# A banded attention and two MLPs in float32: score products without the high-and-low split, other engines for three PSUM copies, one inversion of the softmax sums per pair

## The chip, the cores and the metric

The kernel runs on one core of a Trainium2 chip. That core has a matrix engine (PE in the profile, with its weight loads as PEld), a vector engine (DVE), an activation engine (ACT), a third elementwise engine (POOL) and an engine that issues transfers (SP). Each engine runs its own list of instructions in order, and the lists meet at semaphores. [...]

The metric is the device time of one execution in microseconds, given as the median of several runs. Before the change it is 720.07 us, the median of 3 runs from 719.04 to 720.75 us.

## The reference

```python
def _attn_ref(q, k, v, n_sink, window):        # q, k, v: [2, 8, 768, 64] float32
    scores = scale * np.matmul(q, k.transpose(0, 1, 3, 2))
    keep = is_sink | in_window                 # n_sink = 4, window = 128
    scores = np.where(keep, scores, -1000000000.0)
    scores = scores - np.max(scores, axis=-1, keepdims=True)
    a = np.exp(scores)
    a = a / (np.sum(a, axis=-1, keepdims=True) + 1e-09)
    return np.matmul(a, v)
def _moe_ref(x, w_in, w_out):                  # x: [1536, 512]; w_in [512, 2048]
    h = x @ w_in
    return (h * (1.0 / (1.0 + np.exp(-1.702 * h)))) @ w_out
def _moe2_ref(x, w_gate, w_val, w_out):        # [512, 1536] twice, [1536, 512]
    gate = 1.0 / (1.0 + np.exp(-(x @ w_gate)))
    return (gate * (x @ w_val)) @ w_out
```

The output is the second MLP of the first MLP of the attention's result. The weights come as float64.

## The kernel before

**Products in two formats.** PE takes 4-byte operands in two ways here. In the round format (float32r) an operand carries a shortened mantissa, so the kernel splits a float32 number into a high and a low part and adds three products (high by high, high by low, low by high). In the plain format (float32) one matrix instruction of the program does the whole product. Both MLPs and the scores use the split; the product of the probabilities with v and all transposes are plain.

**Phase A** is the attention. It has 2 batches of 3 query blocks of 256 queries, and each block has 4 pairs of heads, so 24 units. A unit goes through four stages. `st_a` (line 241) transposes q and k of a pair on PE into the PSUM tile `tqk` and brings them to the SBUF tile `kq` of that pair: ACT casts the high part (L255), DVE subtracts it to get the low part (L257), POOL carries the previous block's keys (L246) and the sinks (L259) along. `st_b` (line 262) makes the scores `s` of each half block (`e`) and each head (`j`), with three products each (L278): the two heads of a pair hold 64 rows of PE each. DVE adds the mask and takes the maximum (L283), ACT exponentiates and sums (L291), DVE adds 1e-9 to the sums and inverts them (L294, L295), once for each half block, and POOL scales (L298). `st_c` (line 303) transposes the probabilities (L315) into the PSUM tile `tp`, and ACT copies them to `pt` (L319). `st_d` (line 330) multiplies them with v (L347) and splits the result for the MLP. The first block of a batch has 128 and 256 key columns in its two half blocks, the others 272 each.

**Behind phase A** run the first products of the first MLP, `ha` in `mlp_h` (line 359), one set per block of 256 tokens, and the conversion of weights from float64 (L100 to L108). From some 174 us on, PE does the MLPs alone.

**The order of the work.** The emission order is the string `order` with the four stages at lags 0, 1, 3 and 4 units, but the tile framework reorders it: it simulates a timeline of the whole program and lists each engine's instructions by that. So the lists move wherever an edit changes an instruction's length or engine. PSUM has three buffers for transposes (`ps_t`), three for scores (`ps_s`), one for `o` and one for `ha`.

Of the kernel before, what the change touches and what calls it, by code (L numbers as in the profile page):

```python
# [8 lines left out]
F32 = mybir.dt.float32  # L9
# [6 lines left out]
P = 128  # L16
NS = 16          # sink columns that the banded path carries
NEG = -3.0e38
# the high words of 2^-127 and of the largest float32, both as float64, read as float32
# [19 lines left out]
def fast_path(ctx, tc, ident, nwv, any_, q, k, v, n_sink, window, w_in, w_out, w_gate, w_val, w_out2, out):  # L39
# [5 lines left out]
    KD = DM // P              # 4 contraction tiles of the model dimension  # L45
    TB = 512                  # tokens per MLP block
    NTB = NT // TB
    QB = 256                  # queries per attention block
    NQB = S // QB
    NPAIR = H // 2  # L50
    GF = 4                    # feature tiles per weight group
# [18 lines left out]
    # what the fast path rests on, checked at the end: the sizes of the weights'  # L70
    # exponents, and each row's maximum
# [5 lines left out]
    def weight_block(src, nm, pool):  # L77
        """A block's tiles, and the steps that fill them: float64 words to float32
        (exponent moved, mantissa cut to 24 bits), then hi + lo."""
        wh = pool.tile([P, 4, 512], F32R, tag="wh", name=f"wh_{nm}")  # L80
        wl = pool.tile([P, 4, 512], F32R, tag="wl", name=f"wl_{nm}")

        def load(i):
            raw = stg.tile([P, 512, 2], I32, tag="raw", bufs=2, name=f"raw_{nm}_{i}")
            nc.sync.dma_start(raw, src[:, i, :].bitcast(I32).rearrange("p (f t) -> p f t", t=2))
            return raw

        def steps():
            raws = [load(0)]
            yield  # L90
            for i in range(4):
                if i < 3:
                    raws.append(load(i + 1))
                raw = raws[i]
                lo, hi = raw[:, :, 0], raw[:, :, 1]
                w = stg.tile([P, 512], I32, tag="w", bufs=2, name=f"w_{nm}_{i}")
                wf = w.bitcast(F32)
                n = len(nbig)
                nbig.append(nm)
                nc.scalar.activation(wf, hi.bitcast(F32), AF.Abs, scale=2.0 ** -112,  # L100
                                     accum_out=big[:, n : n + 1])
                yield
                nc.vector.tensor_scalar(w, w, 3, None, ALU.logical_shift_left)
                nc.vector.scalar_tensor_tensor(w, hi, -0x80000000, w, ALU.bitwise_and, ALU.bitwise_or)
                nc.vector.scalar_tensor_tensor(w, lo, 29, w, ALU.logical_shift_right, ALU.bitwise_or)
                yield
                nc.scalar.copy(wh[:, i, :], wf)  # L107
                nc.gpsimd.tensor_tensor(wl[:, i, :], wf, f32(wh[:, i, :]), ALU.subtract)  # L108
                yield

        return (wh, wl), steps()
# [3 lines left out]
    def load_w(src, nm):  # L115
        """The next block, in the slot of the one five before it."""
        w, steps = weight_block(src, nm, wpool if slots[0] % 5 < 3 else wpool2)
        slots[0] += 1
        return w, steps
# [7 lines left out]
    def mm3(ps, ah, al, bh, bl, first, last):  # L127
        """ps += a.T @ b with a = ah + al, b = bh + bl."""
        nc.tensor.matmul(ps, ah, bh, start=first, stop=False)  # L129
        nc.tensor.matmul(ps, ah, bl, start=False, stop=False)  # L130
        nc.tensor.matmul(ps, al, bh, start=False, stop=last)  # L131

    # =====================================================================
    # phase A: attention, with the first weight group behind it
    # =====================================================================
# [31 lines left out]
    def load_vsink(b):  # L167
        """v of the sinks, for the rows (head of the pair, half of the block, sink)."""
        vsk[b] = ap_.tile([4 * NS, NPAIR, 2, D], F32, tag="vsk", bufs=1, name=f"vsk_{b}")
        nc.gpsimd.memset(vsk[b], 0.0)  # L170
        for j in range(2):
            for e in range(2):
                r = (2 * j + e) * NS
                nc.sync.dma_start(vsk[b][r : r + NS, :, e, :],
                                  v[b, j::2, :NS, :].rearrange("h s d -> s h d"))

# [23 lines left out]
    # (their parts stand in a buffer of the probabilities until the masks are made)  # L200
    mt = ap_.tile([P, 2, 2, QB + NS], F32, tag="pr", bufs=2, name="mt").rearrange("p a b c -> p (a b c)")
    rel = mt[:, : QB + P]                             # p - c + 128
# [31 lines left out]
    # keys and queries of a pair of heads, transposed, hi and lo:  # L234
    # previous 128 keys | sinks | own 256 keys | own 256 queries
    C0 = P + NS
    Q0 = C0 + QB
    kq = [kt_p.tile([P, 2, Q0 + QB], F32R, name=f"kq{p}") for p in range(NPAIR)]
    prs, pts, sks = {}, {}, {}

    def st_a(b, t, p):
        """q.T and k.T of a pair of heads, each in two parts."""
        qs, ks = qk[b, t]
        kk = kq[p]
        if t:
            nc.gpsimd.tensor_copy(kk[:, :, :P], f32(kk[:, :, C0 + P : C0 + QB]))  # L246
        tp = ps_t.tile([P, 2, QB], F32, tag="t", name=f"tqk_{b}_{t}_{p}")
        for i, src in enumerate((ks, qs)):
            for c in range(2):
                nc.tensor.transpose(  # L250
                    tp[:, i, c * P : (c + 1) * P], src[:, c, 2 * p : 2 * p + 2, :], ident
                )
        yield
        own = kk[:, :, C0:].rearrange("p s (u c) -> p s u c", u=2)
        nc.scalar.copy(own[:, 0], tp)  # L255
        yield
        nc.vector.tensor_tensor(own[:, 1], tp, f32(own[:, 0]), ALU.subtract)  # L257
        if t == 0:
            nc.gpsimd.tensor_copy(kk[:, :, P : P + NS], f32(kk[:, :, C0 : C0 + NS]))  # L259
        yield  # L260

    def st_b(b, t, p):
        """scores, and their softmax over the kept keys."""
# [5 lines left out]
        for e in range(2):  # L269
            mask = (me, mo)[e] if t else (m0, m1)[e]  # L270
            c0 = (e * P if t else C0)      # the first of the columns of keys
# [3 lines left out]
            for i, (qi, ki) in enumerate(((0, 0), (0, 1), (1, 0))):  # L275
                for j in range(2):
                    hd = slice(64 * j, 64 * j + 64)
                    nc.tensor.matmul(ss[j][:, :n], kq[p][hd, qi, qsl], kq[p][hd, ki, c0 : c0 + n],  # L278
                                     start=i == 0, stop=i == 2)
# [8 lines left out]
            for j in range(2):  # L288
                it = 2 * e + j
                pt = pr[:, j, e, :n]  # L290
                nc.scalar.activation(pt, pt, AF.Exp, bias=nm[:, it : it + 1], scale=-1.0,  # L291
                                     accum_out=st[:, e, 0, j : j + 1])
                yield
            nc.vector.tensor_scalar(st[:, e, 1, :], st[:, e, 0, :], 1e-9, None, ALU.add)  # L294
            nc.vector.reciprocal(st[:, e, 1, :], st[:, e, 1, :])  # L295
            for j in range(2):
                pt = pr[:, j, e, :n]
                nc.gpsimd.tensor_scalar(pt, pt, st[:, e, 1, j : j + 1], 1.0, ALU.mult, ALU.mult)  # L298
# [5 lines left out]
    def st_c(b, t, p):  # L304
        """the probabilities, keys on partitions."""
        pr = prs.pop((b, t, p))
        mine = pts[b, t, p] = []
        for j in range(2):
# [10 lines left out]
            nc.scalar.copy(pt[:, o0:, :], tp[:, o0:, :])  # L319
# [11 lines left out]
    def st_d(b, t, p):  # L331
        """x.T of a pair of heads, in two parts."""
# [27 lines left out]
    def mlp_h(g):  # L360
        """the first weight group's products for one block of QB tokens."""
# [18 lines left out]
    # a pair of heads goes through a, b, c, d in turn; W: weights  # L380
# [29 lines left out]
    # =====================================================================  # L410
    # phase B: the other weight groups of the first MLP
    # =====================================================================
# [75 lines left out]
    def o_stage(g, tb, wo, gs):  # L488
        for j in range(TB // P):
            n = tb * (TB // P) + j  # L490
            ts_ = slice(j * P, (j + 1) * P)
            # the very last tile in halves: the first one leaves while the second is computed
# [14 lines left out]
    def check_inputs():  # L507
        """Does any input leave what the fast path covers?"""
# [14 lines left out]
    # each block's second product runs behind the next block's first tile of features  # L523
# [31 lines left out]
def general_path(ctx, tc, ident, nwv, q, k, v, n_sink, window, w_in, w_out, w_gate, w_val, w_out2, out):  # L555
    """Any n_sink, window, scores and weights: full score rows, plain float32 products."""
# [12 lines left out]
    # keep (1 or 0) for each tile of queries, and (keep - 1) * 1e9  # L569
# [60 lines left out]
    def weights(src, nm):  # L630
        """[128, 4, 512] of float64 to float32, held within float32's range."""
# [98 lines left out]
```

## Time and profile before

| | |
|---|---|
| median of 3 runs | 720.07 us (719.04 to 720.75) |
| the profiled execution, first to last instruction | 719.9 us |
| PE busy | 704.8 us, 98% of the span, 3574 instructions |
| DVE busy | 392.9 us, 55% |
| ACT busy | 304.0 us, 42% |
| POOL busy | 161.3 us, 22% |
| share of PE in the chain that ended last | 80% |

A busy time is the sum of the records of an engine, without overlap. A matrix record is longer than the time for which it holds PE: records follow each other before the earlier ones have ended. What a matrix instruction costs is therefore read from the distance between the start of one and the start of the next. The PE clock in the profile is the share of full speed that was granted: 1.00 is 2.4 GHz and 0.50 is 1.2 GHz.

### The profile page before, as it was taken

The numbers are of one execution on the slowest core, as the hardware profiler recorded it, in microseconds if no ns is written. First come the engines' busy times: TensorE is split into PE (matmuls) and PEld (weight loads), VectorE is DVE, ScalarE is ACT, GpSimd is POOL, SyncE is SP. The second block draws the span as 40 slices with busy tenths as digits, with TensorE's granted clock in tenths as the row PEclk, the third lists the DMA queues.
The fourth block names the chain that finished last, engine by engine and source line by source line (L and its number), as shares of the span: only waits on it lengthen the run. The fifth ranks groups of instructions, "written<-read, shape, count | busy, mean of one in ns | idle before, by whom it ended". The sixth has DMA issues, their size and how long they took to land.

```text
span 719.9 us, 9655 instructions
## 1 busy us (share of the span) xinstructions
PE 704.8 (98%) x3574; PEld 562.1 (78%) x3574; DVE 392.9 (55%) x817; ACT 304.0 (42%) x714; POOL 161.3 (22%) x235
## 2 busy tenths in 40 slices
PE   7999999999999999999999999999998999999995
PEld 4667777778877788888888888888886888888884
DVE  5778766453999847835885781113774225222222
ACT  4787867666664424424443552223441203111110
POOL 4556653332232203101300220001330002000000
PEclk7899999999999999999999999999999999999998
DMA  9754572000333403400420140000441000001101
GB/s 213 157 132 108 149 168 81 2 1 1 102 119 106 141 1 100 135 1 1 145 89 0 60 144 32 1 0 1 147 146 60 0 1 1 0 20 40 39 21 63
DMA packets 49928, 49.08 MB, mean 68 GB/s; under 512 B 39504, under 2 KB 39760, under 8 KB 49872
## 3 DMA queue, kind: packets, MB, share of 16 engines
q1 hardware_dynamic: 49264, 48.24, 23.8%
q8 instruction: 30, 0.49, 0.3%
q14 instruction: 26, 0.21, 0.1%
q10 hardware_dynamic: 544, 0.13, 0.1%
q0 software_dynamic: 64, 0.00, 0.1%
HBM read 45.22 MB, written 3.15 MB: 67 GB/s over the span
## 4 chain that ended last, share of the span: by engine, by line
PE 80%; DVE 7%; DMA 7%; ACT 4%; issue 1%; POOL 1%; ACTq 0%; SPq 0%; POOLq 0%; DVEq 0%
PE s L278 6%; PE o L347 6%; PE g L129 4%; PE y L129 4%; PE y L130 4%; PE o L131 4%; PE o L129 4%; PE g L130 4%; PE o L130 4%; PE y L131 4%; PE g L131 4%; PE v L130 4%; PE v L129 4%; PE v L131 4%; PE tp L315 4%; PE h L129 3%
## 5 line engine op out<-in xcount | busy, mean ns | idle before, releaser
L480 DVE TENSOR_TENSOR sv<-v,sv 128x512 f32<-128x512 f32 x36 | 24.8, 689 | 113.8 <-PE v L131 113.8
L130 PE MATMUL y<-gl,wh_o 128*128 128x512 f32 x192 | 75.2, 393 | 0.3 <-DVE gl L429 0.3
L131 PE MATMUL y<-gh,wl_o 128*128 128x512 f32 x192 | 75.0, 391 | 0.0
L129 PE MATMUL y<-gh,wh_o 128*128 128x512 f32 x192 | 73.0, 394 | 0.9 <-DVE yacc L460 0.5
L479 ACT ACTIVATE sv<-g 128x512 f32<-128x512 f32 x36 | 21.4, 594 | 90.4 <-PE g L131 90.4
L298 POOL TENSOR_SCALAR pr<-pr,st 128x272 f32<-128x272 f32 (+2 forms) x96 | 47.8, 511 | 51.2 <-DVE st L295 23.1
L129 PE MATMUL o<-wh_p,gh_v 128*128 128x512 f32 (+1 forms) x148 | 57.1, 386 | 1.9 <-ACT gh_v L428 1.9
L130 PE MATMUL o<-wl_p,gh_v 128*128 128x512 f32 (+1 forms) x148 | 57.1, 386 | 0.0
L131 PE MATMUL o<-wh_p,gl_v 128*128 128x512 f32 (+1 forms) x148 | 57.1, 387 | 0.0
L129 PE MATMUL g<-xh,wh_g 128*128 128x512 f32 x144 | 57.0, 396 | 0.0
L130 PE MATMUL g<-xl,wh_g 128*128 128x512 f32 x144 | 56.8, 394 | 0.0
L131 PE MATMUL g<-xh,wl_g 128*128 128x512 f32 x144 | 56.7, 394 | 0.0
L131 PE MATMUL v<-xh,wl_v 128*128 128x512 f32 x144 | 56.5, 392 | 0.0
L130 PE MATMUL v<-xl,wh_v 128*128 128x512 f32 x144 | 56.5, 392 | 0.0
L129 PE MATMUL h<-xh,wh_i 128*128 128x512 f32 x144 | 56.5, 392 | 0.0
L129 PE MATMUL v<-xh,wh_v 128*128 128x512 f32 x144 | 56.5, 392 | 0.0
L131 PE MATMUL h<-xh,wl_i 128*128 128x512 f32 x144 | 56.4, 392 | 0.0
L130 PE MATMUL h<-xl,wh_i 128*128 128x512 f32 x144 | 56.4, 392 | 0.0
L428 ACT CAST gh_v<-sv 128x512 fp32r<-128x512 f32 x36 | 22.3, 620 | 78.8 <-DVE sv L480 75.7
L278 PE MATMUL s<-kq 64*128 64x272 f32 (+2 forms) x288 | 52.3, 335 | 1.8 <-DVE kq L257 1.1
L291 ACT ACTIVATE pr<-pr,nmax 128x272 f32<-128x272 f32 (+2 forms) x96 | 47.6, 498 | 14.6 <-DVE nmax L283 13.7
L108 POOL TENSOR_TENSOR wl_p<-w_p,wh_p 128x512 fp32r<-128x512 f32 x12 | 15.9, 1334 | 152.7 <-ACT wh_p L107 152.7
(138 smaller groups left out, 1531.6 us busy)
## 6 DMA issues: line engine op xcount, KB each, us to landing
raw_i<-in_moe_w_in_dram SPq DMA_DIRECT2D x16, 512.0 KB, 4.1
raw_o<-in_moe_w_out_dram SPq DMA_DIRECT2D x16, 512.0 KB, 3.2
raw_g<-in_moe_w_gate_dram SPq DMA_DIRECT2D x12, 512.0 KB, 3.6
raw_v<-in_moe_w_val_dram SPq DMA_DIRECT2D x12, 512.0 KB, 3.6
raw_p<-in_moe_w_out_dram SPq DMA_DIRECT2D x12, 512.0 KB, 3.3
v<-in_v_dram SPq DMA_DIRECT2D x12, 256.0 KB, 5.1
out_dram<-oacc SPq DMA_DIRECT2D x11, 256.0 KB, 2.0
k<-in_k_dram SPq DMA_DIRECT2D x10, 256.0 KB, 4.6
```

What stands on the lines that cost most here:

```text
L108: nc.gpsimd.tensor_tensor(wl[:, i, :], wf, f32(wh[:, i, :]), ALU.subtract)
L129: nc.tensor.matmul(ps, ah, bh, start=first, stop=False)
L130: nc.tensor.matmul(ps, ah, bl, start=False, stop=False)
L131: nc.tensor.matmul(ps, al, bh, start=False, stop=last)
L278: nc.tensor.matmul(ss[j][:, :n], kq[p][hd, qi, qsl], kq[p][hd, ki, c0 : c0 + n], start=i == 0, stop=i == 2)
L291: nc.scalar.activation(pt, pt, AF.Exp, bias=nm[:, it : it + 1], scale=-1.0, accum_out=st[:, e, 0, j : j + 1])
L298: nc.gpsimd.tensor_scalar(pt, pt, st[:, e, 1, j : j + 1], 1.0, ALU.mult, ALU.mult)
L315: nc.tensor.transpose(tp[:, o, :], pr[:, j, e, c0 : c0 + P], ident)
L347: nc.tensor.matmul(o[64 * j : 64 * j + 64, cs], vf(2 * p + j), pf(j), start=i == 0, stop=i == len(steps) - 1,)
L428: nc.scalar.copy(h, src)
L479: nc.scalar.activation(sg, pss[0], AF.Sigmoid)
L480: nc.vector.tensor_tensor(sg, pss[1], sg, ALU.mult)
```

## The change

Four edits in phase A; the diff also strips comments, which is not shown.

- `kq` holds plain float32 and has no low half. A score is one plain product instead of three round ones.
- q.T and k.T leave PSUM by one DVE copy (L254 after) instead of an ACT cast and a DVE subtraction. The two POOL copies of keys have half the size.
- The transposed probabilities of the second head of a pair leave PSUM by DVE instead of ACT (L318 after).
- The softmax sums of both half blocks are inverted in one step, after the last exponential of the pair (L290, L291 after); all scaling on POOL comes behind it.

```diff
-    kq = [kt_p.tile([P, 2, Q0 + QB], F32R, name=f"kq{p}") for p in range(NPAIR)]
+    kq = [kt_p.tile([P, Q0 + QB], F32, name=f"kq{p}") for p in range(NPAIR)]
...
         if t:
-            nc.gpsimd.tensor_copy(kk[:, :, :P], f32(kk[:, :, C0 + P : C0 + QB]))
+            nc.gpsimd.tensor_copy(kk[:, :P], kk[:, C0 + P : C0 + QB])
...
         yield
-        own = kk[:, :, C0:].rearrange("p s (u c) -> p s u c", u=2)
-        nc.scalar.copy(own[:, 0], tp)
+        nc.vector.tensor_copy(kk[:, C0:], tp.rearrange("p u c -> p (u c)"))
         yield
-        nc.vector.tensor_tensor(own[:, 1], tp, f32(own[:, 0]), ALU.subtract)
         if t == 0:
-            nc.gpsimd.tensor_copy(kk[:, :, P : P + NS], f32(kk[:, :, C0 : C0 + NS]))
+            nc.gpsimd.tensor_copy(kk[:, P : P + NS], kk[:, C0 : C0 + NS])
...
-            for i, (qi, ki) in enumerate(((0, 0), (0, 1), (1, 0))):
-                for j in range(2):
-                    hd = slice(64 * j, 64 * j + 64)
-                    nc.tensor.matmul(ss[j][:, :n], kq[p][hd, qi, qsl], kq[p][hd, ki, c0 : c0 + n],
-                                     start=i == 0, stop=i == 2)
+            for j in range(2):
+                hd = slice(64 * j, 64 * j + 64)
+                nc.tensor.matmul(ss[j][:, :n], kq[p][hd, qsl], kq[p][hd, c0 : c0 + n], start=True, stop=True)
...
-                                     accum_out=st[:, e, 0, j : j + 1])
+                                     accum_out=st[:, 0, e, j : j + 1])
                 yield
-            nc.vector.tensor_scalar(st[:, e, 1, :], st[:, e, 0, :], 1e-9, None, ALU.add)
-            nc.vector.reciprocal(st[:, e, 1, :], st[:, e, 1, :])
+        nc.vector.tensor_scalar(st[:, 1], st[:, 0], 1e-9, None, ALU.add)
+        nc.vector.reciprocal(st[:, 1], st[:, 1])
+        yield
+        for e in range(2):
+            n = QB + NS if t else (P if e == 0 else QB)
             for j in range(2):
                 pt = pr[:, j, e, :n]
-                nc.gpsimd.tensor_scalar(pt, pt, st[:, e, 1, j : j + 1], 1.0, ALU.mult, ALU.mult)
+                nc.gpsimd.tensor_scalar(pt, pt, st[:, 1, e, j : j + 1], 1.0, ALU.mult, ALU.mult)
...
-            nc.scalar.copy(pt[:, o0:, :], tp[:, o0:, :])
+            (nc.vector.tensor_copy if j else nc.scalar.copy)(pt[:, o0:, :], tp[:, o0:, :])
```

The lists move as follows. A row is line, operation, tiles (written, then read) and shape; `s_0_3_1_0` is the score tile of block 0, pair 3, half block 1, head 0 (the batch is left out), and `x3` means three equal instructions in a row.

First, PE's list at the very start of the program, before:

```order
L250 MATMUL tqk_0_0_164<-ident,q_0_121 128x128 x2
L250 MATMUL tqk_0_1_172<-ident,k_0_122 128x128
L250 MATMUL tqk_0_2_243<-ident,k_0_122 128x128
L278 MATMUL s_0_0_0_0_180<-kq_156 128x128
L278 MATMUL s_0_0_0_1_181<-kq_156 128x128
L278 MATMUL s_0_0_1_0_214<-kq_156 128x256
L250 MATMUL tqk_0_1_172<-ident,k_0_122 128x128
L250 MATMUL tqk_0_1_172<-ident,q_0_121 128x128
L250 MATMUL tqk_0_2_243<-ident,k_0_122 128x128
L250 MATMUL tqk_0_2_243<-ident,q_0_121 128x128
```

The same place of PE's list after the change:

```order
L250 MATMUL tqk_0_0_164<-ident,q_0_121 128x128 x2
L250 MATMUL tqk_0_1_171<-ident,k_0_122 128x128
L250 MATMUL tqk_0_2_231<-ident,k_0_122 128x128
L275 MATMUL s_0_0_0_0_179<-kq_156 128x128
L275 MATMUL s_0_0_0_1_180<-kq_156 128x128
L275 MATMUL s_0_0_1_0_205<-kq_156 128x256
L250 MATMUL tqk_0_1_171<-ident,k_0_122 128x128
L250 MATMUL tqk_0_1_171<-ident,q_0_121 128x128
L250 MATMUL tqk_0_2_231<-ident,k_0_122 128x128
L250 MATMUL tqk_0_2_231<-ident,q_0_121 128x128
```

The lists read alike, but the three score rows were the high-by-high products, which need the ACT cast alone, and are now whole products, which need the DVE copy; the transposes of pairs 1 and 2 stand behind them in both.

Second, PE's list around the first product with v of block 1 (`o_1_0`), before:

```order
L278 MATMUL s_1_2_0_0_581<-kq_158 128x272 x3
L278 MATMUL s_1_2_0_1_582<-kq_158 128x272 x3
L315 MATMUL tp_1_0_0_564<-ident,pr_1_0_439 128x128 x2
L315 MATMUL tp_1_0_1_597<-ident,pr_1_0_439 128x128 x2
L278 MATMUL s_1_2_1_0_615<-kq_158 128x272 x3
L324 MATMUL ts_1_0_605<-ident,sk_1_0_441 64x128
L278 MATMUL s_1_2_1_1_616<-kq_158 128x272 x3
L315 MATMUL tp_1_1_0_634<-ident,pr_1_1_509 128x128 x2
L347 MATMUL o_1_0_661<-pt_1_0_0_569,v_0_1_301 64x256
```

The same place after the change:

```order
L275 MATMUL s_1_2_0_0_514<-kq_158 128x272
L275 MATMUL s_1_2_0_1_515<-kq_158 128x272
L275 MATMUL s_1_2_1_0_539<-kq_158 128x272
L314 MATMUL tp_1_0_0_497<-ident,pr_1_0_394 128x128 x2
L250 MATMUL tqk_1_3_505<-ident,k_1_226 128x128 x2
L250 MATMUL tqk_1_3_505<-ident,q_1_225 128x128 x2
L314 MATMUL tp_1_0_1_526<-ident,pr_1_0_394 128x128 x2
L314 MATMUL tp_1_0_0_497<-ident,pr_1_0_394 128x128 x2
L314 MATMUL tp_1_0_1_526<-ident,pr_1_0_394 128x128 x2
L346 MATMUL o_1_0_579<-pt_1_0_0_502,v_0_1_278 64x256
L346 MATMUL o_1_0_579<-pt_1_0_1_532,v_0_1_278 64x256
```

Three scores that stood in three groups now stand in one; two score groups and a transpose that stood between the last transpose of `tp_1_0_1` and the product `o_1_0` are gone from there.

Third, DVE's list at that place after the change, where `pt_1_0_1` is what `o_1_0` reads:

```order
L291 RECIPROCAL st_1_0_395<-st_1_0_395 128x4
L356 TENSOR_TENSOR xl_83<-o_0_3_520,xh_80 128x256
L290 TENSOR_SCALAR st_1_1_454<-st_1_1_454 128x4
L291 RECIPROCAL st_1_1_454<-st_1_1_454 128x4
L254 COPY kq_159<-tqk_1_3_505 128x512
L318 COPY pt_1_0_1_532<-tp_1_0_1_526 128x512
L103 TENSOR_SCALAR w_i_2_248<-w_i_2_248 128x512
```

Two PSUM copies that stood in ACT's list now follow each other here, behind the sums of two pairs.

## Rows read from the trace of the kernel before

**Rows 1.** Windows: length, busy (count) of PE, PEld, DVE, ACT, POOL; clock; DMA.

```profile
0.00:23.00 23.00, 18.83 (x75) 12.28 (x75) 14.01 (x58) 11.49 (x35) 12.00 (x31) 0.70 0.97 208
23.00:43.00 20.00, 20.00 (x127) 13.21 (x125) 13.48 (x60) 15.18 (x48) 10.21 (x24) 1.00 0.69 148
...
174.00:720.00 546.00, 535.20 (x2348) 436.49 (x2346) 286.99 (x419) 183.26 (x357) 76.91 (x56) 1.00 0.18 57
```

**Rows 2.** PE timeline, 113 to 116 us: start, length, line, tiles, shape, count.

```profile
113.47 0.64 PE L347 MATMUL o<-pt,v 128*64 128x256 f32 x2
114.04 0.66 PE L278 MATMUL s<-kq 64*128 64x272 f32 x3
114.63 0.65 PE L347 MATMUL o<-pt,v 128*64 128x256 f32 x2
115.20 0.65 PE L278 MATMUL s<-kq 64*128 64x272 f32 x6
115.78 0.44 PE L347 MATMUL o<-pt,v 128*64 128x128 f32 x4
```

**Rows 3.** PE timeline, three short stretches at 79, 91 and 144 us.

```profile
79.11 0.55 PE L278 MATMUL s<-kq 64*128 64x128 f32 x3
79.59 0.65 PE L347 MATMUL o<-pt,v 128*64 128x256 f32 x4
...
90.91 0.61 PE L278 MATMUL s<-kq 64*128 64x256 f32 x3
91.45 0.39 PE L129 MATMUL ha<-xh,wh_i 128*128 128x256 f32 x1
...
143.77 0.43 PE L347 MATMUL o<-pt,v 128*64 128x128 f32 x2
144.13 0.65 PE L347 MATMUL o<-psk,vsk 32*64 32x128 f32 x8
```

**Rows 4.** Groups by form, 0 to 140 us: weight loads, count, busy, mean ns.

```profile
L278 PEld LDWEIGHTS s<-kq 64*128 64x128 f32 x249 | 30.7, 204 | 15.3 <-issue 5.1 <-DVE nmax L283 3.4 <-DVE kq L257 1.7
L315 PEld LDWEIGHTS tp<-ident,pr 128*128 128x128 f32 x136 | 15.6, 145 | 5.5 <-issue 2.3 <-POOL sk L301 0.2 <-POOL kq L246 0.2
L324 PEld LDWEIGHTS ts<-ident,sk 128*64 128x64 f32 x11 | 1.2, 110 | 0.6 <-issue 0.2
```

**Rows 5.** PE timeline, 59 to 63 us.

```profile
59.40 0.39 PE L278 MATMUL s<-kq 64*128 64x272 f32 x1
59.72 0.44 PE L250 MATMUL tqk<-ident,k 128*128 128x128 f32 x2
...
60.74 1.09 PE L347 MATMUL o<-pt,v 128*64 128x256 f32 x12
61.76 0.65 PE L347 MATMUL o<-psk,vsk 32*64 32x128 f32 x8
62.35 0.39 PE L129 MATMUL ha<-xh,wh_i 128*128 128x256 f32 x1
62.57 0.28 PE L130 MATMUL ha<-xl,wh_i 128*128 128x256 f32 x1
62.69 0.28 PE L131 MATMUL ha<-xh,wl_i 128*128 128x256 f32 x1
```

**Rows 6.** DVE: one instruction of tile kq (ns min/median/max), one group by form.

```profile
L257 DVE TENSOR_TENSOR kq<-tqk,kq x24: 664/686/693, 9.0 to 149.6; 128x512 fp32r<-128x512 f32 x24
...
L460 DVE COPY yacc<-y 128x512 f32<-128x512 f32 x12 | 8.1, 678 | 0.0
```

**Rows 7.** Timelines of DVE and PE, the first 14 us.

```profile
8.03 0.14 DVE L513 TENSOR_SCALAR fl<-nwv 128x1 f32<-128x1 f32 x1
8.96 0.69 DVE L257 TENSOR_TENSOR kq<-tqk,kq 128x512 fp32r<-128x512 f32 x1
...
6.76 0.50 PE L278 MATMUL s<-kq 64*128 64x128 f32 x3
9.70 1.22 PE L278 MATMUL s<-kq 64*128 64x128 f32 x6 [1.12 <-DVE kq L257]
```

## The prediction

> **What bounds the kernel now.** I read the page's engine table first: PE is busy for 704.8 of 719.9 us, so any change has to be priced in PE time unless it opens a wait. The windows [rows 1] then cut the span where the change has an end. It touches phase A alone: from 174 us on PE has the MLPs to itself (535.20 busy of 546 us), and these instructions are the same in both kernels. So the question is when PE gets there. The first 23 us are different from the rest: PE is busy for 18.83 of them at a mean granted clock of 0.70, because the clock stands at 1.2 GHz from about 9 us until 22.9 us. From 23 us on the clock is 1.00 and PE has no gap that counts (20.00 busy of 20). DVE is busy for 13.48 and ACT for 15.18 of those 20 us, so neither sets the pace, though neither is far away. Hence two parts: a start in which waits and the clock count, and some 150 us in which the length of PE's own list counts.
>
> The last view is PE's timeline, read from start to start. A lone group of three round products for one score of 272 columns holds PE for 0.59 us (114.04 to 114.63), and a group of six, both heads of a pair, for 0.58 us (115.20 to 115.78) [rows 2]: the second head lies beside the first in the other 64 rows of PE and costs nothing. For 256 columns a lone group takes 0.54 us and for 128 columns 0.48 us [rows 3]. A group also has a price for itself, whatever it holds: a single round product alone takes 0.32 us [rows 5], so two more add about 0.13 each.
>
> **The change part by part.**
>
> *The price of a plain score.* Before shows no plain product in row halves; the nearest rows are the products with v, which are plain and use column halves. Such a product leaves two records, and one head's product alone holds PE for 0.57 us with 256 columns [rows 2] and 0.36 us with 128 [rows 3]. The difference, 0.21 us for 128 columns, is 1.64 ns a column, four cycles of 2.4 GHz; a plain score of 272 columns streams for 0.45 us. The twelve records of a unit's six products (for each head one of 256 and two of 128 columns) take 1.02 us together [rows 5], where 2 x 256 + 4 x 128 columns, one after the other, would need 1.68 us; so two heads in column halves run side by side. From 256 to 272 columns adds 16 x 1.64 ns = 0.03 us. The weights are 128 columns wide for a score and 64 for a product with v; a plain load of 128 columns lasts 145 ns and one of 64 columns 110 ns [rows 4], so between 0 (hidden) and 0.07 us (two loads) comes on top. I take 0.05: 0.57 + 0.03 + 0.05 = 0.65 us for a lone score of 272 columns, 0.60 to 0.67 at the ends. Against 0.58 that is +0.07 (+0.02 to +0.09). For 256 columns 0.62 against 0.54 is +0.08, for 128 columns 0.41 against 0.48 is -0.07. For both heads together I take the same +0.07, on the ground that they lie side by side (rival 1 takes that away). In PE's list after the change I count 67 groups of scores up to the last product with v: 52 with 272 columns (20 of them of several scores, 32 lone), 8 with 256, 7 with 128. That is 52 x 0.07 + 8 x 0.08 - 7 x 0.07 = +3.8 us, with ends of 0.9 and 4.9.
>
> The rows speak against a gain from fewer instructions here: three round products cost less than one plain one as soon as there are more than about 200 columns. On the loads the Trainium skill (TensorE: Matmul & The Clock Gate, Weight-path perf modes) has a rule that speaks against the change too: a fast weight load is on for 128 weights when the input is not FP32, so that plain scores would lose it. The trace does not agree: the round score loads last 204 ns and the plain loads of 128 columns 145 ns [rows 4]. By the rule the sum would gain rival 5's price, by the rows nothing.
>
> *Fewer groups.* The list of before has 77 groups of scores up to the same point, ten more, because scores stood apart that now stand together (three at one place, as the second pair of lists shows). A change between scores and another shape costs a drain and an exposed load: one product alone takes 0.32 us where a further one adds 0.13, some 0.2 us; and the first product after it starts with an exposed load, as `ha` shows with 0.22 us for the first against 0.12 for the next [rows 5], 0.1 us. Ten times 0.3 is -3.0 us. The products with v stand in 40 groups instead of 38, two times 0.2 us, +0.4. Together -2.6 us (-3.1 to -1.6).
>
> *Waits after 23 us.* Before `o_1_0` PE's list now has nothing between the last transposes of `tp_1_0_1` and the product that reads `pt_1_0_1`. The copy of that tile moved to DVE, where it is queued behind the inversions of two pairs and directly behind the 128x512 copy of `kq_159`. Of such a copy from PSUM, rows show 0.68 us on DVE [rows 6]. Behind the waiting product on PE stand the next scores, and everything of DVE and ACT waits for those. So PE stands for one copy and a semaphore each way, near 0.9 us, if the copy starts at once, up to 1.6 if `kq_159` is just ahead of it. In the other 23 units there is work between the transposes and the product. I take +1.0 us in all (0 to +2.5).
>
> *The start.* The first scores need the DVE copy. It stands just ahead of the third `fl` instruction, which ran at 8.03 us [rows 7], so it ends near 8.75 us. Before, the first three products went at 6.76 us on ACT's cast alone, and the other six stood until 9.70 us for DVE's subtraction at 8.96 us [rows 7]. All first scores are thus ready some 0.9 us sooner; but the transposes of pairs 1 and 2, queued behind them, now wait too. At half clock the differences between plain and round are double, about ten groups times a further 0.08, +0.8 us. I take 0 for both together, with -1.5 and +1.5 as the ends: a clock that rises a little sooner or later moves everything behind it.
>
> *The other edits.* DVE loses 24 subtractions of 0.686 us and gains 24 copies of 0.68 and 24 of `pt` (the same shape or three quarters of it, 0.55 to 0.68 us), and loses half of the small sums and inversions; the net of some 7 us lies in the 6.5 us per 20 that DVE has free [rows 1]. ACT loses 24 casts and 24 copies, about 27 us, for which nothing waited after 23 us. One inversion per pair makes the scaling of the first half block wait for the second exponential; units run three apart between scores and transposes, so PE has other work. POOL copies half as much for the keys. All at nothing; cover gone means rival 4.
>
> *Sum.* 3.8 - 2.6 + 1.0 + 0 = +2.2 us. The profiled execution took 719.9 us, 0.2 below the median of 720.07; I forecast 722.3 us.
>
> **The rivals.**
>
> 1. *The two heads do not run side by side.* Row halves are shown in the round format alone, plain products side by side in column halves alone. If plain products in row halves follow each other, 29 scores that stand second or later in a group cost 0.45 us each, +13: 735 us. Slower; 6%.
> 2. *The start shortens.* Both of PE's waits at 7.93 to 9.70 us shrink, pair 1's keys come sooner (DVE's copy waits for one product set, not three), and the clock rises some 4 us sooner, which saves about 2 us; the sum of PE stays at +1.2 or under, and `o_1_0` finds its tile ready. 2.0 + 1.5 saved against 1.2: about 718. Against it: the granted clock rose only after a long dense stretch, and PE's load there is not lighter. It decides if the rise comes before 20 us. Faster; 18%.
> 3. *The list costs nothing.* Loads of plain scores hidden (0.9) and no new wait: -1.0 to 0.9, so 719 to 721, say 720.5. No change; 22%.
> 4. *DVE sets the pace between 23 and 83 us.* It was busy for 13.48 of 20 us, and gets the `pt` copies, each in a chain transposes, copy, product. If five or six units stand as `o_1_0` does, +5: 726 us. Slower; 12%.
> 5. *The plain load is slow.* At most a whole load of 0.145 us exposed per group, 67 x 0.145 = +9.7: 732 us. Slower; 3%. This is the result that the Trainium skill's rule on fast loads, cited above, would give; the trace's 204 against 145 ns speaks against it.
>
> **How the numbers follow.** The forecast has 39%, its own range 721 to 724.5 us; the rivals have 6, 18, 22, 12 and 3%. The range that should hold 8 of 10 runs from 717.5 to 727, which leaves out rivals 1 and 5 and the far ends of 2. A measurement of this kernel tells 0.2%, 1.44 us, from no change, so the border lies at 718.6 and 721.5 us. Faster: rival 2, and a little of 3, 19%. Same: the rest of 3 and the low end of the forecast, 26%. Slower: the rest, 55%.
>
> **What would show it.** Right: the score line has 192 records (two for each plain score) instead of 288; lone scores of 272 columns hold PE for some 0.65 us and two heads for no more; PE stands near 0.9 us at `o_1_0`; DVE's busy time is near 400 us, ACT's near 277; the clock is at 1.00 from 20 to 26 us on; the MLP stretch is as long as before and begins some 2 us later. Wrong: two heads near 1.1 us (rival 1), a clock at full before 20 us (rival 2), waits of PE for DVE that sum to over 3 us after 23 us (rival 4), a lone score near 0.60 (rival 3) or over 0.75 (rival 5).

## The result, and the profile after

The changed kernel takes 730.24 us, the median of 4 runs (730.14 to 731.40); the kernel before took 720.13 us beside it. The ratio is 1.0126, interval 1.0081 to 1.0171. The forecast was 722.3 us with a range to 727.0: the sign was right, the size was missed by 8 us, and the time lies outside the range. The profiled execution took 728.4 us.

Three windows of the trace after answer to [rows 1]: length, busy time (count) of PE, PEld, DVE, ACT and POOL, granted clock, DMA share, GB/s.

```profile
0.00:23.00 23.00, 17.84 (x59) 9.80 (x59) 11.68 (x53) 7.89 (x26) 10.02 (x30) 0.67 0.97 206
23.00:43.00 20.00, 20.00 (x80) 11.32 (x79) 10.54 (x36) 9.12 (x29) 6.32 (x12) 0.69 0.41 95
43.00:63.00 20.00, 18.86 (x138) 13.16 (x137) 17.12 (x52) 14.08 (x44) 13.65 (x26) 1.00 0.57 143
```

Read the clock column first. In the 20 us from 23 us on the clock was 1.00 before; now it is 0.69, though PE is busy for all 20. PE gets 80 records done there where it had 127 (a plain score leaves two where there were three). Between 43 and 63 us PE has 1.14 us without a record (such a time is called a stand below), and DVE is busy for 17.12 of the 20. In the first 23 us PE's stands sum to 5.16 us (23.00 - 17.84), against 4.17 before (23.00 - 18.83) [rows 1].

The finer windows of the same trace show when the clock came back:

```profile
6.00:8.00 2.00, 0.00 (x0) 0.00 (x0) 1.53 (x9) 0.00 (x0) 0.15 (x1) 0.98 1.14 242
8.00:10.00 2.00, 1.28 (x6) 0.93 (x6) 1.77 (x11) 0.00 (x0) 1.34 (x3) 0.50 1.14 237
...
32.00:34.00 2.00, 2.00 (x10) 1.32 (x7) 0.34 (x2) 0.75 (x2) 0.00 (x0) 0.50 0.13 53
34.00:36.00 2.00, 2.00 (x13) 1.68 (x11) 2.00 (x4) 0.99 (x4) 1.27 (x1) 0.69 0.00 0
36.00:38.00 2.00, 2.00 (x11) 0.82 (x7) 0.50 (x3) 0.13 (x1) 1.60 (x5) 1.00 0.00 0
```

PE runs at 1.2 GHz from 8 us until some 35 us; before, from 9 until 22.9 us. In full-clock time lost that is (1 - 0.67) x 23 + (1 - 0.69) x 20 = 13.8 us against (1 - 0.70) x 23 = 6.9 us [rows 1].

PE's timeline after, at five places (start, length, line, tiles, shape, count; in brackets the idle time ahead and what ended it):

```profile
8.72 1.65 PE L275 MATMUL s<-kq 64*128 64x128 f32 x6 [3.25 <-DVE kq L254]
...
13.75 2.96 PE L275 MATMUL s<-kq 64*128 64x128 f32 x12 [0.57 <-DVE kq L254]
...
112.61 0.70 PE L275 MATMUL s<-kq 64*128 64x256 f32 x2
113.23 0.44 PE L314 MATMUL tp<-ident,pr 128*128 128x128 f32 x2
...
115.06 0.73 PE L275 MATMUL s<-kq 64*128 64x256 f32 x4
115.72 0.38 PE L129 MATMUL ha<-xh,wh_i 128*128 128x256 f32 x1
...
119.66 0.72 PE L275 MATMUL s<-kq 64*128 64x272 f32 x2
120.31 0.39 PE L131 MATMUL ha<-xh,wl_i 128*128 128x256 f32 x1
...
184.54 0.40 PE L129 MATMUL h<-xh,wh_i 128*128 128x512 f32 x1
```

From start to start, a lone plain score of 256 columns takes 0.62 us, both heads together 0.66, and a lone one of 272 columns 0.65. For the lone ones these are the forecast prices to the hundredth; both heads take 0.04 us more than forecast. The MLPs alone begin at 184.54 us, where before they began at 174.48: 10.1 us late, of which the last part of the kernel gave 1.5 back. The loss lies in phase A alone. The stretch ahead of the MLPs as one window, before and after:

```profile
0.00:174.48 174.48, 170.11 (x1232) 126.07 (x1233) 106.44 (x399) 121.20 (x359) 84.40 (x179) 0.96 0.44 104
0.00:184.54 184.54, 178.12 (x1137) 118.48 (x1137) 110.39 (x375) 100.51 (x310) 79.64 (x179) 0.93 0.41 99
```

PE's stands there sum to 4.37 us before and 6.42 after, 2.1 us more: 1.0 of them in the first 23 us, 1.1 behind.

The place around `o_1_0`, on PE, DVE, ACT and POOL (four views of the trace after, same columns):

```profile
47.38 1.62 PE L346 MATMUL o<-pt,v 128*64 128x256 f32 x12 [0.25 <-ACT pt L318]
49.73 0.30 PE L323 MATMUL ts<-ident,sk 128*64 128x128 f32 x1 [0.73 <-POOL sk L300]
```

```profile
46.31 0.69 DVE L254 COPY kq<-tqk 128x512 f32<-128x512 f32 x1 [0.21 <-PE tqk L250]
47.17 0.69 DVE L318 COPY pt<-tp 128x512 f32<-128x512 f32 x1 [0.17 <-PE tp L314]
```

```profile
46.75 0.59 ACT L318 COPY pt<-tp 128x512 f32<-128x512 f32 x1 [1.12 <-PE tp L314]
```

```profile
47.00 2.07 POOL L297 TENSOR_SCALAR pr<-pr,st 128x272 f32<-128x272 f32 x4
49.02 0.95 POOL L300 COPY sk<-pr 128x32 f32<-128x32 f32 x3
```

PE does stand here, as forecast, but 0.25 us for ACT's copy and then 0.73 us for POOL's sinks, which come behind four scalings that now follow the pair's single inversion. DVE's copy of `pt` ended at 47.86 us, and no stand of PE is put down to it; the forecast had 0.9 us.

### The profile page after: what moved, and what is told of

Read it like the earlier page. It is cut to its first block, busy times and chain, and to the rows that moved or that the text cites. A ratio compares the mean times of both kernels' runs of the same rounds, so it can differ in the third digit from the quotient of the medians.

```text
span 728.4 us, 9336 instructions
## 1 busy us (share of the span) xinstructions
PE 712.7 (98%) x3478; PEld 554.1 (76%) x3478; DVE 398.1 (55%) x793; ACT 283.5 (39%) x666; POOL 156.6 (21%) x235
## 4 chain that ended last, share of the span: by engine, by line
PE 80%; DVE 10%; DMA 4%; ACT 3%; POOL 1%; issue 1%; SPq 0%; ACTq 0%; POOLq 0%; DVEq 0%
PE s L275 7%; PE o L346 6%; PE g L129 4%; PE o L131 4%; PE y L129 4%; PE y L130 4%; PE o L129 4%; PE y L131 4%; PE g L130 4%; PE o L130 4%; PE g L131 4%; PE v L131 4%; PE v L130 4%; PE v L129 4%; PE tp L314 3%; PE h L129 3%
## 5 line engine op out<-in xcount | busy, mean ns | idle before, releaser
L275 PE MATMUL s<-kq 64*128 64x272 f32 (+2 forms) x192 | 54.5, 454 | 3.8 <-DVE kq L254 3.8
L297 POOL TENSOR_SCALAR pr<-pr,st 128x272 f32<-128x272 f32 (+2 forms) x96 | 45.3, 492 | 43.5 <-DVE st L291 30.8
```

The costliest lines, as they stand in the source:

```text
L275: nc.tensor.matmul(ss[j][:, :n], kq[p][hd, qsl], kq[p][hd, c0 : c0 + n], start=True, stop=True)
L297: nc.gpsimd.tensor_scalar(pt, pt, st[:, 1, e, j : j + 1], 1.0, ALU.mult, ALU.mult)
```

## The experiments

A cost of half clock is needed to read them. The runs of the kernel before that stood beside the first four experiments took 719.70 us at a mean clock of 0.988, 727.39 at 0.976 and 730.23 at 0.972: 10.5 us for 0.016, so 0.01 of mean clock is 6.6 us. (A straight line through the 70 executions of that kernel, on four chips, whose mean clock is under 0.994 gives 5.5.) Times are ratios to the kernel before on the same chip. "Half" is the time at 1.2 GHz that the clock column of the profiled execution shows ahead of the MLPs, summed from windows of 1 us, and "first h" the start of the MLPs alone.

Two limits of "half" are to be kept in mind. It comes from one execution, and the mean clock of one and the same kernel differs between executions: from 0.971 to 0.989 in those 70 of the kernel before. And the column can miss a stretch: ten more executions of that kernel list 0.995 to 0.998 at 720.8 to 725.3 us, no faster than the others, and so does one of the changed kernel (0.997 at 730.27 us; its other three have 0.978 to 0.980). `b_both` below shows such a stretch.

| run | ratio (interval) | half, us | first h, us |
|---|---|---|---|
| before | 1 | 13.7 | 174.5 |
| changed | 1.0126 (1.0081 to 1.0171) | 27.3 | 184.5 |
| a_fill14 | 1.0058 (1.0023 to 1.0092) | 3.4 | 178.3 |
| b_fill14 | 1.0088 (1.0036 to 1.0140) | 10.2 | 177.6 |
| a_firstact | 1.0086 (1.0049 to 1.0123) | 20.5 | 181.7 |
| a_ptact | 1.0161 (1.0071 to 1.0250) | 27.3 | 189.2 |
| a_fill7 | 1.0124 (1.0082 to 1.0165) | 23.9 | 184.0 |
| b_fill7 | 0.9989 (0.9971 to 1.0006) | 6.8 | 172.6 |
| b_ptdve | 0.9978 (0.9958 to 0.9998) | 17.1 | 174.0 |
| b_both | 1.0153 (1.0113 to 1.0192) | 10.2 in the column, some 21 more by the records | 185.0 |
| a_round0 | 1.0023 (0.9992 to 1.0054) | 13.7 | 177.2 |
| b_plain0 | 0.9997 (0.9962 to 1.0032) | 10.2 | 173.6 |
| a_sums | 1.0151 (1.0115 to 1.0187) | 27.3 | 186.4 |
| a_scores | 1.0143 (1.0098 to 1.0188) | 17.1 | 182.7 |
| a_fillo2 | 729.29 us, one run | 13.7 | 181.8 |
| a_round01 | 736.14 us, one run | 30.7 | 187.4 |
| a_round23 | 741.41 us, one run | 44.4 | 194.6 |
| p_fill7 | 0.9966 (0.9951 to 0.9981) | 10.2 | 172.3 |

**a_fill14, b_fill14**: PE's stand at the start filled.

```diff
+        if (b, t, p) == (0, 0, 0):
+            kb = qs[:, 1, 0:2, :].rearrange("p h d -> p (h d)")
+            for _ in range(14):
+                nc.tensor.matmul(wps.rearrange("p a b -> p (a b)")[:, :P], ident, kb, start=True, stop=True)
```

> The changed kernel with 14 more plain products of 128 columns on PE, behind the first transposes, whose result nobody reads; they fill the 3.25 us for which PE stood before the first scores. Theory (the clock): of the 10.1 us by which the first h product came later, 12.2 us more at half clock make 6.1; if the stand at the start is what brings the fall, the clock stays at 1.00 or comes back some 10 us sooner and the time falls by 5 to 8 us, to 722 to 725. Rival 1 (the clock falls anyway, by the gaps at 12.9 and 20.4 us): the granted clock is at half until about 35 us again, time 729 to 731. Rival 2 (the time is in the list and in waits after 35 us, the clock matters little): the clock changes and the time moves by under 2 us.

> The kernel before with the same 14 products. Theory: its own 13.6 us at half clock are shortened in the same way, at most by 6.8 us: 714 to 717, or 720 where the clock falls anyway at the next gap. Rival 2: 720 in any case. If both kernels keep full clock, the distance between them is the cost of list and waits alone, which the theory puts at 4 us and rival 2 at 9 to 10.

In the changed kernel half clock shrank from 27.3 to 3.4 us and the ratio from 1.0126 to 1.0058. That is some 5 us where the clock alone should give 9 to 11; and the kernel before lost time with the same products. The 14 products also moved the scheduler's list (71 groups of scores where the changed kernel has 67 and the kernel before 77), so these two runs changed two things. Hence the repeats with 7, which leave the other rows in their order:

**a_fill7, b_fill7**: the same edit with 7.

> The changed kernel with 7 plain products of 128 columns on PE behind the first transposes, whose result nobody reads; with 7 all other rows of PE's list stay in their order (with 14 they moved, and the time the clock gave back was lost again to other groups). They take some 1.5 of the 3.25 us for which PE stood. Theory (half clock from 8.0 to 35.1 us cost 5.5 to 6 us against before, and the stand at the start brings it): the half clock starts later and is shorter by 4 us or more, and each us of it less takes 0.45 us off: 724 to 728. Rival (the stands at 12.9 and 20.4 us hold it down): half until 34 to 36 us as in the changed kernel, 729.5 to 730.5.

> The kernel before with the same 7 products; the rest of PE's list stays as it was. Theory: of its 13.6 us at half clock some go, 716 to 720. Rival (the clock of this stretch is not ruled by the stand at the start): 720 to 722.

Theory failed on the changed kernel: the fall of the clock came later, at 10.8 us, but the return stayed near, at 34.7, and no time was won. Half clock was shorter by 3.4 us, worth 1.5 by the runs above, less than the interval tells. On the kernel before half clock halved, and the ratio is within noise. So in these two runs the filled stand moved the fall (7.9 to 10.8 us in the changed kernel, 9.3 to 13.6 in the kernel before) by more than the return (35.2 to 34.7, and 22.9 to 20.4).

**a_firstact**: the first pair's copy on ACT.

```diff
-        nc.vector.tensor_copy(kk[:, C0:], tp.rearrange("p u c -> p (u c)"))
+        (nc.scalar.copy if (b, t, p) == (0, 0, 0) else nc.vector.tensor_copy)(kk[:, C0:], tp.rearrange("p u c -> p (u c)"))
```

> The changed kernel, but the q.T and k.T of the very first pair leave PSUM by ACT, which was free there from 3.1 us on; so the first scores start near 6.3 us instead of 8.7. Theory: PE stands 2.4 us less at the start, and the half clock ends sooner; 722 to 727. Rival 1 (later gaps hold the clock down): 728 to 730, the clock at half until 33 us or more. Rival 2: 727.5 to 728.5, the 2 us of the start alone.

The first scores started at 6.76 us again, and still the clock came back only at 30 us. By the point values a third of the loss went; the intervals overlap, and the list moved (69 groups of scores).

**a_ptact, a_sums**: one edit undone each (`nc.scalar.copy` for both heads; one inversion per half block).

> The changed kernel with all copies of the transposed probabilities on ACT again. Theory: the waits of PE for DVE's copy between 43 and 63 us (1.1 us in the windows) go, the clock is as in the changed kernel: 728 to 730. Rival (DVE is behind the whole loss, by copies queued behind its other work): 721 to 725.

> The changed kernel with one inversion per half block again. Theory: the single inversion matters little by itself; the clock is at half to 33 us or later as in the changed kernel; 77 groups of scores instead of 67 make the list longer by 5 us or more, and the waits of 2.7 us between 43 and 60 us shrink: 731 to 736. Rival (the late scaling after the pair's inversion makes those waits, and they are the loss): 724 to 728.

Half clock is that of the changed kernel in both. PE's stands between 36 and 60 us are gone in `a_ptact` (24.00 busy of 24, against 22.86), but its list has 79 groups of scores instead of 67 (`a_sums`: 77), and both are slower than the changed kernel's point value, within its interval. Undoing either edit alone does not take the loss away.

**b_ptdve, b_both**: the copies of the second head on DVE in the kernel before; the same with one inversion per pair.

```diff
-            nc.scalar.copy(pt[:, o0:, :], tp[:, o0:, :])
+            (nc.vector.tensor_copy if j else nc.scalar.copy)(pt[:, o0:, :], tp[:, o0:, :])
```

> The kernel before with one edit of the change: the transposed probabilities of the second head leave PSUM by DVE. Scores stay round, in three products. PE's list has 67 groups of scores instead of 77. Theory (a group less is worth 0.3 us or more, and DVE's copies cost PE under 1.5 us of waits): list 3 to 6.5 us shorter, waits 0 to 1.5, the time 714.5 to 719 with the clock as before. Rival (waits for DVE eat it): 720 to 724, with waits of PE for DVE pt in the trace.

> The changed kernel with round scores: before plus the copies of the second head on DVE plus one inversion per pair. 65 groups of scores. Its distance to the changed kernel is the price of plain scores and of their start. Theory: list 3 to 5 us shorter than before, waits as in the changed kernel (near 3 us): 716 to 721, so the plain scores cost 9 to 14 us of the change. Rival (plain scores cost nothing, the moved copies and the inversion are behind the loss): 726 to 731.

`b_ptdve` has 67 groups of scores, ten fewer than before, and won 0.2% where the list alone had promised 3 to 6.5 us. Windows of it, where before has 20.00 in the first:

```profile
23.00:43.00 20.00, 19.47 (x142) 13.28 (x142) 15.56 (x64) 14.67 (x48) 9.99 (x24) 0.95 0.73 156
43.00:63.00 20.00, 19.05 (x160) 15.30 (x162) 17.66 (x52) 15.89 (x48) 12.97 (x20) 1.00 0.39 117
```

PE now stands for 1.5 us in these 40, where it stood for 0.2. The first h came 0.45 us sooner than before, with 1.8 us more of stands ahead of it (167.85 us busy of 174.03) and 3.4 us more at half clock, some 1.6 us. What is left, some 3.9 us, is the shorter list: it came as forecast and was spent on stands and clock. In this run a list with fewer groups had less in it to fill waits with, so the two terms of my sum are not independent. `b_both` refutes my expectation outright: with round scores the two other edits cost as much as the whole change. Its windows:

```profile
23.00:43.00 20.00, 19.13 (x124) 12.97 (x124) 12.98 (x49) 13.22 (x43) 9.37 (x19) 1.00 0.49 121
43.00:63.00 20.00, 18.11 (x114) 14.28 (x115) 14.37 (x36) 11.21 (x35) 11.27 (x18) 0.74 0.50 124
63.00:83.00 20.00, 18.89 (x154) 14.41 (x154) 16.48 (x47) 15.75 (x46) 14.68 (x21) 1.00 0.60 160
```

PE stands for 3.9 us in these 60, 1.5 of them at once for POOL's conversion of a weight, and the clock falls behind that stand. Ahead of 27 us the clock column shows 1.00 throughout, but the records do not bear it out:

```profile
6.48 0.69 PE L250 MATMUL tqk<-ident,k 128*128 128x128 f32 x2 [0.84 <-DMA k<-in_k_dram]
...
9.75 1.22 PE L278 MATMUL s<-kq 64*128 64x128 f32 x6 [0.50 <-DVE kq L257]
...
25.01 1.54 PE L350 MATMUL o<-pt,v 128*64 128x256 f32 x6
...
35.21 0.86 PE L350 MATMUL o<-pt,v 128*64 128x256 f32 x6
```

The same six records of products with v take 1.54 us at 25.01 and 0.86 at 35.21. The six of scores take 1.22 us, as they do before at 9.70 us [rows 7], where the clock was 0.50, and the two transposes at 6.48 us take 0.69 us where before, at 6.39 us and full clock, they took 0.44. By these lengths PE ran at 1.2 GHz until some 27 us, some 21 us that the column lacks. With the 10.2 us that it shows, that is some 17 us of half clock more than before, worth some 8 of the 11 us. So `b_both` loses at half clock for the most part, like the changed kernel, and with round scores.

**a_scores**: of the change only the plain scores with the DVE copy of q.T and k.T.

> Of the change only the plain scores with the DVE copy of q.T and k.T; probabilities by ACT, one inversion per half block. C1: half clock to 28 us or later here too; list 2 us longer than the changed kernel's, waits under 1.5 us: 727 to 732. Rival (pt on DVE and the single inversion are behind the loss): 718 to 723.

By itself this edit is as slow as the change, with half clock for 17.1 us only: the theory held in its time but not in the clock's end (26.4 us). Half clock for 3.4 us more than before is worth 1.6 of its 10 us. Most of the rest is its list: PE has 296 groups of all kinds ahead of the MLPs, where the changed kernel has 281 and the kernel before 275.

**a_round0, b_plain0**: the format of the first block's scores alone.

```diff
-            for j in range(2):
+            if (b, t) == (0, 0):
+                for i in range(3):
+                    for j in range(2):
+                        hd = slice(64 * j, 64 * j + 64)
+                        nc.tensor.matmul(ss[j][:, :n], kq[p][hd, qsl], kq[p][hd, c0 : c0 + n], start=i == 0, stop=i == 2)
+            for j in range(2 if b + t else 0):
                 hd = slice(64 * j, 64 * j + 64)
-                nc.tensor.matmul(ss[j][:, :n], kq[p][hd, qsl], kq[p][hd, c0 : c0 + n], start=True, stop=True)
+                nc.tensor.matmul(ss[j][:, :n], f32(kq[p][hd, qsl]), f32(kq[p][hd, c0 : c0 + n]), start=True, stop=True)
```

> The changed kernel, with the 16 scores of the very first block as three round products each (all three of the unsplit operands, so the low halves are left out and the values of that block are wrong); kq is written in the round format and read as plain by the other blocks. PE's list is nearly that of the changed kernel. Theory C1 (half clock to 35 us comes from the plain scores of the first block): full clock is back by 21 to 26 us, lists and waits later stay, and the time falls by some 0.45 us for each of 9 to 14 us: 724 to 727. Rival C2 (the start, one hop for DVE and the stands on it, brings it, whatever the format): full clock at 33 to 36 us, 729 to 731.

> The kernel before, with the 16 scores of the very first block as one plain product each of the high halves (the two other products of that block are left out). C1: half clock lasts until 28 us or later instead of 22.9, and the time is 722 to 728 though the list is not longer. C2: half clock ends at 20 to 24 us as before, 717 to 721.

The diff is that of `a_round0` (`kq` in the round format, and what reads it as plain on POOL, is not shown); `b_plain0` does the reverse in the kernel before. `a_round0` has nearly the changed kernel's list and the same late start, and its loss is gone but for 0.2%. PE's timeline and clock:

```profile
8.95 1.65 PE L277 MATMUL s<-kq 64*128 64x128 f32 x9 [1.75 <-DVE kq L254]
...
13.77 3.07 PE L277 MATMUL s<-kq 64*128 64x128 f32 x18 [0.57 <-DVE kq L254]
```

```profile
20.00:22.00 2.00, 2.00 (x8) 1.05 (x6) 2.00 (x8) 1.51 (x4) 1.42 (x3) 0.52 0.53 101
22.00:24.00 2.00, 2.00 (x17) 1.33 (x17) 2.00 (x9) 1.82 (x8) 0.88 (x1) 1.00 1.15 250
```

The scores start as late as in the changed kernel, and yet full clock is back at 21.9 us instead of 35. Its first h comes 2.75 us later than before, with 1.1 us of it in stands, so 1.6 are left for the list; the changed kernel's comes 7.3 us later still. So the long half clock carries most of the loss. But `b_plain0` (its list moved too) speaks against plain scores as such: half clock there was 10.2 us, shorter than before. And `b_both`, with round scores, was at half clock until 27 us.

**a_fillo2, a_round01, a_round23**: one look each at what holds the clock down.

```diff
+            if (b, t, p, j) == (0, 0, 0, 1):
+                for _ in range(2):
+                    nc.tensor.matmul(wps.rearrange("p a b -> p (a b)")[:, :P], ident, pr[:, 0, 1, P : 2 * P], start=True, stop=True)
```

> The changed kernel with two plain products of 128 columns, whose result nobody reads, between the last transposes of the first pair and the first product with v, so that PE has no stand of 0.14 us at 20.4 us. Theory (the plain scores of the first block keep the clock at half, whatever the stands): full clock at 30 us or later. Rival (that stand does it): full clock by 26 us.

> The changed kernel with round scores (three products of the unsplit operands, low halves left out) for pairs 0 and 1 of the very first block alone. Theory (it is the plain scores that follow the last stand, those of pairs 2 and 3 among them): full clock between 22 and 30 us. Rival (only the first two pairs count, since they stand next to the waits): by 22 us, as with all four.

> The same for pairs 2 and 3 of the very first block alone. Theory: full clock between 21 and 28 us, at least 7 us sooner than the changed kernel's 35. Rival (only the first two pairs count): 33 to 36 us.

With two products in the stand of 0.14 us at 20.4 us, all scores plain, full clock was back at 21.8 us:

```profile
19.71 1.06 PE L317 MATMUL wps<-pr,ident 128*128 128x128 f32 x4
20.57 0.63 PE L314 MATMUL tp<-ident,pr 128*128 128x128 f32 x2
21.13 0.94 PE L349 MATMUL o<-pt,v 128*64 128x256 f32 x2
```

```profile
20.00:22.00 2.00, 2.00 (x9) 1.09 (x8) 0.65 (x5) 1.42 (x5) 1.40 (x4) 0.56 0.59 117
```

That is the rival. `a_round0` had no stand there either, and `a_fill7` and `a_ptact`, which came back at 34 to 35 us, had it. But `a_round01` had none between 12.9 us and its return at 30.1 (behind stands of 0.46 and 0.38 us at 42 to 44 us its clock fell again, from 50.6 to 60.9), `a_firstact` none and came back at 30.2, `a_sums` none and came back at 34.8; `a_round23` had one of 0.14 us at 20.1 and came back at 53.4; and `a_fill14` had one of 0.14 us at 17.5 and came back at 18.7. So the absence of that stand does not suffice, and a stand need not bring a late return. The three runs here (of the last two the diff, that of `a_round0` with `p < 2` and `p > 1`, is not shown) are one execution each, and executions of one kernel differ in their clock, so none of them shows a cause by itself. Besides, `a_fillo2` moved the list behind its products (75 groups of scores) and won little by its clock.

**p_fill7**: `b_ptdve` with the 7 products of `b_fill7`.

> The kernel before with the second head's copies on DVE and with the 7 products at the start, the rest of PE's list as in the run of those copies alone. Theory: both small gains add, 0.2% from the copies and 0.1% from the later fall of the clock: ratio 0.995 to 0.998. Rival (the gains are noise): 0.999 to 1.002.

The point values of both gains add (that of the 7 products alone is within noise), to 0.34% (0.19 to 0.49): the lowest ratio of all runs. Its first 23 us (PE, clock 0.66 over 15 us where the copies alone had 0.50):

```profile
8.00:23.00 15.00, 13.96 (x68) 9.80 (x68) 12.41 (x54) 9.89 (x34) 8.62 (x21) 0.66 1.05 239
```

## Why the prediction was wrong

- **The price of a plain score: right.** 0.65 and 0.62 us measured for a lone one, and 0.66 for both heads: they cost as one. Rival 1 is out, and so is rival 5. The prediction's reading of the loads (204 against 145 ns) set two shapes against each other, and a stretch at half clock was in it. Loads of one shape, from 40 to 140 us, before and after:

```profile
L278 PEld LDWEIGHTS s<-kq 64*128 64x128 f32 x171 | 19.6, 185 | 9.1 <-issue 3.1 <-DVE nmax L283 1.9 <-DVE st L295 0.6
L275 PEld LDWEIGHTS s<-kq 64*128 64x128 f32 x118 | 14.4, 185 | 8.2 <-issue 3.2 <-DVE nmax L279 1.1 <-DVE w_i L104 0.4
```

  A load took 185 ns in both formats, so the loads of plain scores lost nothing. By the Trainium skill (TensorE: Matmul & The Clock Gate, Weight-path perf modes) loads of 128 weights that are not FP32 would be the fast ones; these rows show no difference.
- **Rivals 2 to 4 did not come**: the clock rose later, not sooner; the list was no cheaper; the stands of PE for DVE stayed far under 3 us.
- **Waits after 23 us: right in size, other in make-up.** PE has 1.14 us without a record between 36 and 60 us, near the +1.0. But the largest is not for DVE: it is the 0.73 us for POOL, where the prediction put the single inversion at nothing because "PE has other work". Here it had none.
- **The step that failed: "I take 0 for both together, with -1.5 and +1.5 as the ends".** Half clock doubled from 13.7 to 27.3 us. 13.8 - 6.9 = 6.9 us of full clock more are lost, 0.0095 of the span, and at 6.6 us for 0.01 that makes 6.3 of the 10 us (5.2 at the flatter 5.5). The prediction knew that a later rise would move everything behind it, priced the shift at 1.5 us and looked only at an earlier one (rival 2). At half clock the price runs as long as the clock stays down; the end had to be as far as it might stay down. The same term covered PE's stands at the start, which grew by 1.0 us: the first scores came at 8.72 us, as forecast, but behind one stand of 3.25 us.
- **The other 3.8 us** are 2.1 us of stands (1.0 at the start, 1.1 behind) and some 1.7 us of a longer list, near the 1.6 us of `a_round0`. The list term was +1.2 (3.8 - 2.6), and so nearly right. It counted the groups of scores and of products with v alone: ten groups of scores went, but transposes of probabilities stand in 69 groups instead of 62 and `ha` in 56 instead of 51, and groups of all kinds ahead of the MLPs are 281 instead of 275. That the term came out near is in part luck.
- **Fewer groups: the mechanism holds, the independence does not.** Ten groups of scores fewer made the list of `b_ptdve` some 3.9 us shorter, but came with 1.5 us of stands, and in the reverse runs `a_ptact` and `a_sums` more groups came with fewer stands.
- **What stays open:** what makes the chip grant full clock at 22 us in one list and at 35 in the next. `a_round0` and `a_fillo2` each brought it back 13 us sooner; `b_plain0` and `b_both` forbid to call the format the cause, `a_sums`, `a_round01` and `a_fill14` the stand. Nor does one list fix the time: executions of the kernel before differ among themselves in their clock. And the list moves with nearly every edit, so that the costs of the edits do not add: `a_scores` and `b_both` each cost as much as all four, the first mostly by its list, the second mostly at half clock.

## What to carry to other kernels

When a kernel's first stretch runs at half clock, give that stretch its own rival with a price of about half of each further us, and an end as far as the clock could stay down: here it was worth more than all prices of instructions behind it. Check the clock column by the lengths of equal records before you rely on it. Where a scheduler writes the lists, an experiment is clean only if the rest of the list stays in its order; choose the size of the edit so that it does. And groups saved on the busiest engine need not be free: in `b_ptdve` stands came in their place.

## What the runs showed of the hardware

- The price of time at 1.2 GHz was 6.6 us for 0.01 of mean clock, from runs of one and the same kernel (719.70 us at 0.988, 730.23 at 0.972), and 5.5 us by the line through 70 runs.
- The clock column of a trace can lack a stretch: in `b_both` it shows 1.00 at 25 us, where six records take 1.54 us that take 0.86 at 35 us.
- A weight load of a score (64x128) takes 185 ns in the round and in the plain format.
- Plain products of two heads in the two row halves of PE run side by side: 0.66 us for both, 0.62 us for one, of 256 columns each.
- Two products of 128 columns, 0.86 us at half clock (19.71 to 20.57), in a stand of 0.14 us went with a return to full clock 13 us sooner, in one run.
- A DVE copy of 128x512 from PSUM takes 0.69 us where the same copy on ACT takes 0.59 (`pt` at 47.17 and 46.75 us).
